# One-hot rows of the first batch turned as words of two tokens, and another order of the queues up to FFN block 1

## The chip, the cores and the metric

The kernel runs on 1 core of one Trainium2 chip. The metric is the time of one execution on the device in microseconds; lower is better. The engines are named as in the profile: PE (TensorE, with its weight loads as PEld), DVE (VectorE), ACT (ScalarE), POOL (GpSimd) and SP (SyncE, which here issues nearly all DMAs).

## The reference

Routed attention in which a query sees only the keys of its own cluster, followed by a feed-forward block (FFN) with a SoLU and a layer norm. There are 4 batches, 8 heads, 768 tokens, head size 64, 16 clusters; the FFN goes from 512 to 1024 and back over 3072 tokens.

```python
q_assign = argmax(einsum('bhsd,hcd->bhsc', q_n, c_n), axis=-1)   # k_assign alike, rows normalised
mask = q_assign[:, :, :, None] == k_assign[:, :, None, :]
scores = np.where(mask, scale * q @ k.T, -1e9)
attn = softmax(scores, axis=-1)
x = (attn @ v) with heads side by side           # 3072 x 512
h = x @ w_in
solu = h * softmax(h, axis=-1)
ln = (solu - mean) / sqrt(var + 1e-6) * g_ln
out = ln @ w_out
```

## The kernel before, in words

**Masking by product.** The mask is not applied afterwards. For each token a one-hot row of its cluster (16 rows, and 32 partitions are kept) is placed under the 64 rows of q and of k in the tiles `qbig` and `kbig`. A score product over 80 partitions then gives q.k/256 plus 1 where the clusters agree, and the exponential (`expo`, line 643, ACT, `scale` 256/8 and `bias` minus that) brings everything else to about zero. So before any score of a pair of heads can be formed, its q and k have to be loaded, turned, cast, assigned to clusters, and their one-hot rows placed.

**Names.** The work is a list of named operations, each with an engine. For batch b and pair p of heads (i is 0 for q, 1 for k):
- `ld b.p.i` loads tokens (SP), `tp` turns them on PE (batch 0 only, two halves of 384 columns into PSUM banks), `xa`/`xt` copies the two halves from PSUM to the tile `xt` (in later batches `xt` is one DVE transpose).
- `ca b.p.i.hh` casts `xt` to bf16 into `qbig`/`kbig` (lines 436 to 440; hh is the head of the pair; pair 0 of batch 0 in halves).
- `cl` multiplies by the centroids on PE (line 469), `tb` turns the result on DVE into `cst` (line 478), `mx` takes the maximum over 16 clusters (line 488), `oh` compares with it and gives the one-hot tile `oh` (line 492), `ot` turns that back into `oht` (lines 499 and 504), `pl` places its rows under q and k (lines 528 and 530, four per item). Pair 0 of batch 0 goes in two items, `0.0` and `0.0.1`, of 192 columns; pairs 1 to 3 of batch 0 are one item of 384 columns each.
- `S r.x` are score products into the PSUM tiles `sb` (line 633), four products a region r; `E r` is the exponential of region r; `V n.j` are the products with the values into the bank `ob` (line 655); `N g` normalises (lines 667 and 678, DVE). In batch 0 the regions S0 to S8 belong to pair 0, and S9, S12 and S15 are the first ones of pairs 1, 2 and 3.
- `lv`/`cv` load and cast v; `lo`/`me`/`mk`/`mf`/`km`/`ce` centre the second weight matrix once (`gt`, `gk`, `gw` prepare g_ln for it); `li` loads the first one. `h`, `hm`, `ex`, `u`, `tu`, `bn`, `y`, `sc`, `ou` are the FFN of one block of 128 tokens, spread between the scores of later batches; `tx` turns its input.

**What sets the order.** One list, `ORDER`, names every operation once; operations are recorded in that order, so each engine's queue is the list with the other engines' names left out. An engine takes its queue strictly in order and stands still when the next operation's inputs are missing. A table, `AWAY`, moves single operations to another engine than their usual one. PE and ACT are tied by a ring: two `sb` tiles of 1024 columns hold scores, so S of region r waits for E of region r-2, and E waits for its S.

**Token order of batch 0.** A partition of the loaded tile holds six neighbouring tokens (6c to 6c+5). Turned by PE, tokens come in groups of 128 with step six. In the `qbig`/`kbig` of batch 0 column j*256 + q*128 + c holds token 6c + 2j + q. A score product takes 128 neighbouring columns as keys; in later batches keys are every sixth column.

Of the kernel before, what the change touches and what calls it, by code (L numbers as in the profile page):

```python
# [38 lines left out]
lc ld0.0.0.0 ld0.0.1.0 ld0.0.0 ld0.0.1 wu ld0.1.0 ld0.1.1 ld0.2.0 cx cy lv0.0 ld0.2.1 tp0.0.0.0 cz  # L39
ld0.3.0 tp0.0.0.1 xa0.0.0 lg tp0.0.1.0 xt0.0.0 ca0.0.0.0.0 lv0.1 cp lo1 ca0.0.0.0.1 cb tp0.0.1.1  # L40
xa0.0.1 ld0.3.1 ca0.0.0.1.0 ca0.0.1.0.0 cl0.0 cc lo2 xt0.0.1 ca0.0.0.1.1 tp0.1.0.0 tb0.0
ca0.0.1.1.0 tp0.1.0.1 mx0.0 xa0.1.0 cl0.0.1 ca0.0.1.0.1 oh0.0 xt0.1.0 tp0.1.1.0 ca0.0.1.1.1 tb0.0.1
ld1.0.0.0 tp0.1.1.1 xa0.1.1 ca0.1.0.0 mx0.0.1 ot0.0 ld1.0.0.1 xt0.1.1 tp0.2.0.0 oh0.0.1 pl0.0.1.1
# [129 lines left out]
def kernel(  # L173
# [15 lines left out]
    P = 128  # L189
# [293 lines left out]
    def each(x, t):  # L483
        return x[:, :wide(t)].rearrange("p (a c) -> p a c", c=NC_)
# [863 lines left out]
```

## Time and profile before

| | |
|---|---|
| Time, median of 3 runs | 221.01 us (220.79 to 221.11) |
| Profiled execution, its own time | 221.75 us |
| Span of that execution in the trace | 219.9 us |
| ACT busy | 191.6 us, 87% of the span |
| DVE busy | 185.4 us, 84% |
| POOL busy | 159.7 us, 73% |
| Granted clock of PE | 1.0 in all stretches |

The time of an execution is a little longer than its span, since the span counts from the first to the last instruction. In rows of the timeline the columns are: start, length in us, engine, line of the kernel, operation, output and input tile with partitions x elements and type, and the number of instructions merged into the row; in brackets the idle time of the engine ahead of the row and who ended it. In rows of groups the number behind the comma is the mean of one instruction in ns. An engine's row can be longer than the time until the next one begins, as neighbouring instructions overlap.

### The profile page before, as it was taken

To read this page: it belongs to the slowest core of one execution; us is meant where nothing else is said; L and a number is where in the kernel's file an instruction comes from. 1 tells how busy PE (TensorE), PEld (TensorE's weight loads), DVE (VectorE), ACT (ScalarE), POOL (GpSimd) and SP (SyncE) were. 2 spreads that over 40 slices of the span, in tenths; PEclk is the share of its full clock that TensorE was granted. 3 is DMA by queue.
4 is the path that set the end of the run, shared out by engine and by line. 5 is a ranking of instruction groups with operands and counts; after the bars stand their busy time and mean duration, and the time that the engine had idled before them with its cause. 6 is when DMAs were issued, how large, how long until landed. Compare 5 with 4: busy or idle time off the path is not lost.

```text
span 219.9 us, 6271 instructions
## 1 busy us (share of the span) xinstructions
PE 210.8 (96%) x2400; PEld 148.0 (67%) x2431; DVE 185.4 (84%) x431; ACT 191.6 (87%) x242; POOL 159.7 (73%) x199
## 2 busy tenths in 40 slices
PE   7799989999999999999999999999999999999993
PEld 4467657777768777877677677666777766655552
DVE  3799989879799999996899999994888756889892
ACT  3599989999999999999999989999999888785471
POOL 3699688859898999649939987979989054456530
PEclk9999999999999999999999999999999999999999
DMA  6995999998199999999989991919474329686613
GB/s 190 381 368 137 281 183 182 169 162 190 23 194 174 208 167 150 217 249 210 185 198 168 190 171 23 221 48 214 140 167 97 84 48 187 137 135 145 190 51 145
DMA packets 120879, 37.28 MB, mean 170 GB/s; under 512 B 109961, under 2 KB 116369, under 8 KB 120849
## 3 DMA queue, kind: packets, MB, share of 16 engines
q1 hardware_dynamic: 119872, 35.31, 77.7%
q0 software_dynamic: 544, 1.05, 2.9%
q10 hardware_dynamic: 432, 0.52, 0.7%
q8 instruction: 19, 0.31, 0.6%
q14 instruction: 12, 0.09, 0.1%
HBM read 23.11 MB, written 6.29 MB: 134 GB/s over the span
## 4 chain that ended last, share of the span: by engine, by line
PE 87%; DVE 6%; DMA 3%; issue 2%; SPq 1%; POOL 0%; ACT 0%; DVEq 0%
PE sb L633 27%; PE hb L766 18%; PE mb L838 16%; PE ob L655 15%; PE hb L469 4%; DMA raw<-in_q_dram 3%; PE hb L395 2%; PE hb L838 2%; DVE oht L504 1%; PE mb L469 1%; DVE mx L488 1%; DVE cst L478 1%; DVE qbig L530 1%; DVE xt L408 1%; PE sb L838 0%
## 5 line engine op out<-in xcount | busy, mean ns | idle before, releaser
L643 ACT ACTIVATE e<-sb 128x1024 bf16<-128x1024 f32 x144 | 140.3, 1022 | 9.8 <-PE sb L633 8.8
L633 PE MATMUL sb<-qbig,kbig 80*128 80x256 bf16 (+3 forms) x648 | 84.9, 261 | 1.0 <-POOL kbig L530 0.4
L633 PEld LDWEIGHTS <-kbig 80*128 80x128 bf16 (+1 forms) x648 | 62.4, 119 | 24.7 <-issue 6.5
L799 POOL TENSOR_TENSOR u<-e_sb,w_st 128x1024 bf16<-128x1024 bf16 x21 | 45.0, 2143 | 18.6 <-ACT e_sb L792 12.1
L655 PEld LDWEIGHTS <-e 128*128 128x128 bf16 x1152 | 48.6, 97 | 12.7 <-issue 2.3
L655 PE MATMUL ob<-v,e 128*128 128x65 bf16 x1140 | 51.8, 193 | 0.4 <-DVE x L678 0.2
L766 PE MATMUL hb<-w_in_sb,xT 128*128 128x512 bf16 x172 | 50.4, 379 | 0.6
L838 PE MATMUL mb<-w_out_c,uT 128*128 128x512 bf16 x157 | 43.6, 379 | 0.6
L810 DVE BATCH_NORM_STATS2 bs<-u 128x6 f32<-128x512 bf16 x48 | 31.8, 681 | 1.1 <-POOL u L799 1.0
L792 ACT ACTIVATE e_sb<-w_st,nmax 128x1024 bf16<-128x1024 f32 (+1 forms) x25 | 27.8, 1113 | 5.5 <-DVE w_st L776 4.1
L438 POOL CAST qbig<-xt 64x768 bf16<-64x768 f32 (+1 forms) x31 | 25.8, 834 | 6.4 <-ACT xt L406 2.2
L440 POOL TENSOR_SCALAR kbig<-xt 64x768 bf16<-64x768 f32 (+1 forms) x30 | 26.7, 894 | 2.2 <-DVE xt L420 0.7
L834 POOL TENSOR_TENSOR alpha<-var,halves 128x1 f32<-128x1 f32 x24 | 15.7, 655 | 11.8 <-DVE var L817 11.2
L420 DVE STREAM_TRANSPOSE xt<-raw 128x768 f32<-128x768 f32 x24 | 22.6, 960 | 0.0
L838 PEld LDWEIGHTS <-uT 128*128 128x128 bf16 x176 | 15.2, 97 | 9.6
L766 PEld LDWEIGHTS <-xT 128*128 128x128 bf16 x192 | 16.1, 98 | 7.9
L776 DVE TENSOR_SCALAR_CACHE_REDUCE w_st<-hb,nmax 128x512 f32<-128x512 f32 x24 | 17.9, 744 | 2.9 <-PE hb L766 2.3
L678 DVE TENSOR_TENSOR x<-ob,den 128x256 bf16<-128x256 f32 (+2 forms) x40 | 19.0, 474 | 1.4
L776 DVE TENSOR_SCALAR_CACHE_REDUCE w_st<-hb 128x512 f32<-128x512 f32 x24 | 16.3, 680 | 3.9 <-PE hb L766 3.8
L667 DVE RECIPROCAL den<-ob 128x4 f32<-128x4 f32 (+2 forms) x40 | 7.2, 180 | 9.7 <-PE ob L655 9.2
L530 POOL COPY qbig<-oht 32x768 f32<-32x768 f32 (+2 forms) x11 | 9.2, 837 | 8.4 <-DVE oht L499 7.3
L530 POOL COPY kbig<-oht 32x768 f32<-32x768 f32 (+2 forms) x17 | 11.1, 654 | 3.2 <-DVE oht L504 2.0
(114 smaller groups left out, 203.0 us busy)
## 6 DMA issues: line engine op xcount, KB each, us to landing
vf<-in_v_dram SPq DMA_DIRECT2D x16, 384.0 KB, 4.9
out_dram<-y SPq DMA_DIRECT2D x20, 256.0 KB, 3.6
raw<-in_k_dram SPq DMA_DIRECT2D x26, 192.0 KB, 3.8
raw<-in_q_dram SPq DMA_DIRECT2D x24, 192.0 KB, 5.1
w_g<-in_moe_w_out_dram SPq DMA_DIRECT2D x4, 512.0 KB, 7.3
raw<-in_q_dram SPq DMA_DIRECT2D x3, 384.0 KB, 7.0
raw<-in_k_dram SPq DMA_DIRECT2D x3, 384.0 KB, 7.4
w_in_sb<-in_moe_w_in_dram POOLq DMA_DIRECT2D x2, 512.0 KB, 7.4
```

Source lines behind the costliest of these rows:

```text
L420: nc.vector.transpose(xts[b, p, i][:], raw_of(b, p, i))
L438: (nc.vector if e == "DVE" else nc.gpsimd).tensor_copy(dst, src)
L440: (nc.vector if e == "DVE" else nc.gpsimd).tensor_scalar(dst, src, scalar1=inv_C, scalar2=1.0, op0=Alu.mult, op1=Alu.mult)
L633: nc.tensor.matmul(reg[:, c:c + wd], kb[u, pp, side_of(h), keys], qb[u, pp, side_of(h), su * P:su * P + wd])
L643: nc.scalar.activation(es[r][:, :w], src, Act.Exp, scale=exp_scale, bias=-exp_scale)
L655: nc.tensor.matmul(ops_of(group_of[n])[:, s, :VW], es[r][:, c0:c0 + P], v1[index[b, pair_of(h)] % R][:, side_of(h), kt, :VW], start=(kt == ...
L766: nc.tensor.matmul(hb[f2][:], xTs[f][:, dc, :], w_in_sb[:, dc, f2 * BANK:(f2 + 1) * BANK], start=(dc == 0), stop=(dc == n_dc - 1))
L776: nc.vector.tensor_scalar(ff[f, "h"][:, f2 * BANK:(f2 + 1) * BANK], hb[f2][:], scalar1=-1.0, scalar2=nmax[:, f2 - 1:f2] if f2 else 3.0e38, ...
L792: nc.scalar.activation(ff[f, "e"][:, cols(f, f2)], ff[f, "h"][:, cols(f, f2)], Act.Exp, bias=ff[f, "nmax"][:, n_ff2 - 1:], scale=-1.0, acc ...
L799: (nc.vector if e == "DVE" else nc.gpsimd).tensor_tensor(ff[f, "u"][:, cols(f, f2)], ff[f, "e"][:, cols(f, f2)], ff[f, "h"][:, cols(f, f2) ...
L810: nc.vector.bn_stats(ff[f, "bs"][:, f2, :], ff[f, "u"][:, f2 * BANK:(f2 + 1) * BANK])
L838: nc.tensor.matmul(y_of(f, x), ff[f, "uT"][:, fc, :], w_out_c[:, fc, parts_of(f, x)], start=(fc == 0), stop=(fc == n_fc - 1))
```

## The change

It has two parts.

**Words of two tokens.** In batch 0 the two tokens 6c + 2j and 6c + 2j + 1 now lie side by side: column j*256 + 2c + q. `oh` writes its one-hot values with the two tokens' bits of a cluster next to each other, so that two bf16 values form one 4-byte word, and `ot` turns words: one transpose of half as many elements in place of two transposes of 2-byte elements. The casts of batch 0 write every second column; score products of batch 0 load every second column as keys; a block of 128 outputs of batch 0 holds 64 pairs of neighbouring tokens, so the store goes by pairs of rows.

```diff
-            dst = (big_[:D, pp, x].rearrange("p (j q a c) -> p a j q c", q=2, a=2, c=D)
+            dst = (big_[:D, pp, x].rearrange("p (j a c q) -> p a j q c", q=2, a=2, c=D)
...
-            dst = big_[:D, pp].rearrange("p h (j q c) -> p h j q c", q=2, c=P)[:, :, :, hh]
+            dst = big_[:D, pp].rearrange("p h (j c q) -> p h j q c", q=2, c=P)[:, :, :, hh]
...
     def assign_hot(t):
         asg[t, "oh"] = pr.tile([P, 2 * HALF], BF16, name="oh")
+        if early(pairs[ITEMS[t][0][0]][0]):
+
+            w = wide(t)
+            nc.vector.tensor_tensor(
+                asg[t, "oh"][:, :w].rearrange("p (k c q) -> p k q c", q=2, c=NC_),
+                asg[t, "cst"][:, :w].rearrange("p (k q c) -> p k q c", q=2, c=NC_),
+                asg[t, "mx"][:, :w // NC_].rearrange("p (k q) -> p k q", q=2).unsqueeze(3)
+                .to_broadcast([P, w // NB, 2, NC_]), op=Alu.is_ge)
+            return
...
-        for x in range(2):
-            nc.vector.transpose(
-                asg[t, "oht"][:, :2 * w].rearrange("p (j q c) -> p j q c", j=n_t // 2, q=2)[:, :, x],
-                asg[t, "oh"][:, :w].rearrange("p (k q c) -> p k q c", q=2, c=NC_)[:, :, x]
-                .unsqueeze(2).to_broadcast([P, w // NB, 2, NC_]))
+        nc.vector.transpose(
+            asg[t, "oht"][:, :2 * w].bitcast(F32),
+            asg[t, "oh"][:, :w].bitcast(F32).rearrange("p (k c) -> p k c", c=NC_)
+            .unsqueeze(2).to_broadcast([P, w // NB, 2, NC_]))
...
-            src = asg[t, "oht"][r, :2 * L].bitcast(F32).rearrange("p (t c) -> p t c", c=NB)
+            src = asg[t, "oht"][r, :2 * L].bitcast(F32).rearrange("p (j c) -> p j c", c=D)
             dst = (big_[D:HOT, pp, c0 // HALF].bitcast(F32)
-                   .rearrange("p (t a c) -> p t a c", a=2, c=NB)[:, :, x])
+                   .rearrange("p (j a c) -> p j a c", a=2, c=D)[:, :, x])
...
-            keys = bass.ts(kt, P) if early(b) else slice(kt, S, n_t)
+            keys = (slice(kt // 2 * 2 * P + kt % 2, (kt // 2 + 1) * 2 * P, 2) if early(b)
+                    else slice(kt, S, n_t))
...
-            dst = out[b * S:(b + 1) * S].rearrange("(p t) m -> t p m", t=n_t)[su]
+
+            dst = (out[b * S:(b + 1) * S].rearrange("(g p j q) m -> j g p q m", g=2, j=n_t // 2, q=2)
+                   [su // 2, su % 2])
+            o = ff[f, "o"][:]
+            eng.dma_start(out=dst.rearrange("p q m -> p (q m)"), in_=o)
+            return
```

**Order and engines.** `ORDER` changes from the first loads up to the scores of batch 1 that run beside FFN block 1 (about S60); behind that every engine's queue is as before. 35 operations change engine, 30 of them in batch 0's preparation:

```diff
-    ca0.0.1.0.0 ca0.3.0.1 ca3.1.1.0 ca3.2.0.1 cv0.0.0 cv0.0.1 cv0.1.1 cv1.1.0 cv1.1.1 cv1.2.0
+    ca0.0.1.0.1 ca0.1.1.0 ca3.1.1.0 ca3.2.0.1 cv0.1.0 cv1.1.0 cv1.2.0 cv1.3.1 cv2.0.1 cv2.1.0
```

To DVE go ca0.0.0.0.0, ca0.0.0.1.0, ca0.0.0.1.1, ca0.1.0.1, ca0.2.0.0, xa0.1.1, xa0.2.0, pl0.0.1.1.1, pl0.1.1.0, pl0.2.0.0, cv0.3.1, ce1 and ce6. To ACT go xt0.0.0, xt0.0.1, xt0.2.1, ca0.0.1.0.1, ca0.1.1.0, cv0.1.0, pl0.0.1.1, pl0.0.0.0, pl0.0.1.1.0 and pl0.2.1.1. To POOL go ca0.0.1.0.0, ca0.3.0.1, pl0.0.1.0, pl0.0.1.0.1, pl0.2.0.1, cv0.0.0, cv0.0.1, cv0.1.1, cv0.3.0, cv1.1.1, ce2 and ce4. On SP the load of g_ln goes ahead of the second k load of pair 2, one load of w_out (lo0) and v of pair 2 go ahead of batch 1's first loads, and v of pair 3 goes ahead of four loads of batch 1's k.

The queue of PE, where the first score products (into `sb_90`) stand between turns of tokens (into the banks `hb_92` and `hb_93`) and pair 1's centroid products (into `mb`). Before:

```order
L395 MATMUL hb_92<-ident_f,raw 128x128 x3
L395 MATMUL hb_93<-ident_f,raw 128x128 x3
L469 MATMUL mb<-xt,g_wide 32x384 x4
L633 LDWEIGHTS kbig_99
L633 MATMUL sb_90<-qbig_96,kbig_99 128x256
```

After, at the same place:

```order
L394 MATMUL hb_92<-ident_f,raw 128x128 x3
L641 LDWEIGHTS kbig_99
L641 MATMUL sb_90<-qbig_96,kbig_99 128x256
...
L468 MATMUL mb<-xt,g_wide 32x384 x4
L394 MATMUL hb_93<-ident_f,raw 128x128 x3
```

The first scores moved ahead of pair 1's centroid products and of one turn of tokens.

The queue of DVE while pair 0's two items are assigned (`cst`, `mx`, `oh`, `oht` as above; `kbig_99` and `qbig_96` are the tiles of pairs 0 and 1). Before:

```order
L478 STREAM_TRANSPOSE cst<-mb 128x192
L488 TENSOR_REDUCE mx<-cst 128x12
L440 TENSOR_SCALAR kbig_99<-xt 64x2x3x64
L492 TENSOR_TENSOR oh<-cst,mx 128x192
L478 STREAM_TRANSPOSE cst<-mb 128x192
L488 TENSOR_REDUCE mx<-cst 128x12
L504 STREAM_TRANSPOSE oht<-oh 128x3x64 x2
L492 TENSOR_TENSOR oh<-cst,mx 128x192
L504 STREAM_TRANSPOSE oht<-oh 128x3x64 x2
L530 COPY qbig_96<-oht 32x6x32
```

After:

```order
L477 STREAM_TRANSPOSE cst<-mb 128x192
L487 TENSOR_REDUCE mx<-cst 128x12
L494 TENSOR_TENSOR oh<-cst,mx 128x6x2x16
L511 STREAM_TRANSPOSE oht<-oh 128x192
L477 STREAM_TRANSPOSE cst<-mb 128x192
L407 COPY xt<-hb_92 128x384
L487 TENSOR_REDUCE mx<-cst 128x12
L494 TENSOR_TENSOR oh<-cst,mx 128x6x2x16
L511 STREAM_TRANSPOSE oht<-oh 128x192
L537 COPY kbig_99<-oht 32x3x64
```

The first item's turn now follows its comparison at once and is one instruction; the cast between left, and a copy of a turned half came in.

The queue of DVE from pair 3's `cst` on, to the placing of its rows (`kbig_100` and `qbig_97` are the tiles of pairs 2 and 3). Before:

```order
L478 STREAM_TRANSPOSE cst<-mb 128x384
L530 COPY kbig_100<-oht 32x384
L667 RECIPROCAL den<-ob 128x4
L678 TENSOR_TENSOR x<-ob,den 128x2x2x64
L488 TENSOR_REDUCE mx<-cst 128x24
L492 TENSOR_TENSOR oh<-cst,mx 128x384
L440 TENSOR_SCALAR kbig_100<-xt 64x6x128
L504 STREAM_TRANSPOSE oht<-oh 128x3x128 x2
L530 COPY qbig_97<-oht 32x384
```

After:

```order
L477 STREAM_TRANSPOSE cst<-mb 128x384
L537 COPY qbig_97<-oht 32x384
L675 RECIPROCAL den<-ob 128x4
L686 TENSOR_TENSOR x<-ob,den 128x2x2x64
L537 COPY kbig_100<-oht 32x384
L487 TENSOR_REDUCE mx<-cst 128x24
L439 TENSOR_SCALAR kbig_100<-xt 64x768
L494 TENSOR_TENSOR oh<-cst,mx 128x12x2x16
L511 STREAM_TRANSPOSE oht<-oh 128x384
L537 COPY qbig_97<-oht 32x384
```

Both placings of pair 2 that DVE does now stand behind `cst` of pair 3, one of them behind a normalisation; the cast of pair 3's keys moved ahead of the comparison, and the turn is one instruction.

More of the change, by code (lines that the diff above doesn't have):

```diff
@@ L35 @@
+    u19.0 u2.0 u21.0 u22.0 u3.0 u4.0 u5.0 u6.0 u7.0 u8.0 u9.0
 """.split(), "POOL"))
 ORDER = """
[L39 to L43, printed above, removed]
```

113 lines of the change are left out of this document (58 added, 55 removed).

## The prediction

> **What bounds the kernel now.** I read the page first, then the busy time of every engine in stretches, then the waits of PE, and last the timeline of each engine around those waits.
>
> ```profile
> span 219.9 us, 6271 instructions
> PE 210.8 (96%) x2400; PEld 148.0 (67%) x2431; DVE 185.4 (84%) x431; ACT 191.6 (87%) x242; POOL 159.7 (73%) x199
> PE 87%; DVE 6%; DMA 3%; issue 2%; SPq 1%; POOL 0%; ACT 0%; DVEq 0%
> ```
>
> PE is busy 96% of the span and carries 87% of the chain that ended last. The change takes no product away from PE, so the gain can be no more than idle time of PE. The table by stretches (columns: length, then busy time and instructions of PE, weight loads, DVE, ACT, POOL) says where that idle time lies:
>
> ```profile
> 5.00:10.00 5.00, 3.82 (x38) 2.56 (x37) 3.69 (x11) 2.91 (x7) 3.35 (x8) 1.00 1.02 365
> 10.00:12.16 2.16, 1.92 (x17) 0.81 (x15) 2.06 (x8) 1.85 (x5) 1.44 (x5) 1.00 1.06 399
> 20.00:25.00 5.00, 4.85 (x70) 2.95 (x68) 4.81 (x13) 4.64 (x7) 3.97 (x7) 1.00 0.99 302
> 25.00:30.00 5.00, 4.58 (x54) 2.68 (x51) 4.78 (x10) 4.56 (x6) 3.25 (x7) 1.00 1.00 161
> 30.00:35.00 5.00, 4.59 (x71) 3.58 (x70) 3.99 (x8) 4.56 (x5) 4.84 (x8) 1.00 1.16 203
> 40.00:45.00 5.00, 4.82 (x67) 3.38 (x67) 4.01 (x9) 4.83 (x6) 3.09 (x4) 1.00 0.99 160
> 50.00:55.00 5.00, 4.95 (x59) 3.71 (x58) 4.61 (x12) 5.00 (x7) 4.64 (x7) 1.00 0.78 173
> 120.00:160.00 40.00, 39.58 (x440) 28.09 (x447) 35.33 (x80) 38.25 (x49) 35.04 (x39) 1.00 0.78 145
> ```
>
> PE idles 1.18 us in 5 to 10, 0.24 in 10 to 12.16, 0.15 in 20 to 25, 0.42 in 25 to 30, 0.41 in 30 to 35 and 0.18 in 40 to 45. From 45 on it loses about 1% (0.42 of 40 us in 120 to 160), and there every queue but the order of a few entries stays as it was. These are the waits behind the sums:
>
> ```profile
> PE ob L655 <- DVE x L678: 0.2, 1, 0.2
> 8.10 0.87 PE L395 MATMUL hb<-ident_f,raw 128*128 128x128 f32 x6 [0.41 <-DMA raw<-in_q_dram]
> 10.48 0.93 PE L395 MATMUL hb<-ident_f,raw 128*128 128x128 f32 x6 [0.24 <-ACT xt L406]
> 12.16 0.60 PE L633 MATMUL sb<-qbig,kbig 80*128 80x256 bf16 x4
> 29.06 0.61 PE L633 MATMUL sb<-qbig,kbig 80*128 80x256 bf16 x4 [0.42 <-POOL kbig L530]
> 33.07 0.60 PE L633 MATMUL sb<-qbig,kbig 80*128 80x256 bf16 x4 [0.32 <-ACT e L643]
> ```
>
> The first scores (S0) start at 12.16. S15, the first scores of pair 3, wait 0.42 us for the keys' one-hot rows (line 530), and at 33.07 S19 waits 0.32 us for an exponential. The 0.41 at 8.10 and the rest of the 1.18 wait for loads of q and k whose issues keep their places: not recoverable. What the change could at most win is 0.24 + 0.15 + 0.42 + 0.41 + 0.18 = 1.4 us.
>
> **The one-hot turn.** S15 waits because DVE is late with pair 3's one-hot rows:
>
> ```profile
> 10.19 0.63 DVE L504 STREAM_TRANSPOSE oht<-oh 128x192 bf16<-128x192 bf16 x2
> 27.24 1.02 DVE L504 STREAM_TRANSPOSE oht<-oh 128x384 bf16<-128x384 bf16 x2
> 7.76 0.38 DVE L478 STREAM_TRANSPOSE cst<-mb 128x192 f32<-128x192 f32 x1
> 17.17 0.57 DVE L478 STREAM_TRANSPOSE cst<-mb 128x384 f32<-128x384 f32 x1
> 28.32 1.24 POOL L530 COPY kbig<-oht 32x384 f32<-32x384 f32 x2 [1.42 <-DVE oht L504]
> ```
>
> The turn of pair 3 ends at 28.26, POOL's placing starts at 28.32, and PE goes at 29.06. Two 2-byte turns become one turn of 4-byte words with half the elements. The nearest rows of that type and size are the f32 turns of line 478: 0.38 us for 192 elements and 0.57 for 384. I take those: 2 x (0.63 - 0.38) + 3 x (1.02 - 0.57) = 1.9 us less on DVE before 28 us. If a word cost as much as two 2-byte elements, nothing would be won; no row speaks for that.
>
> **DVE's moved work.** Between its first cst and pair 3's turn DVE gives away two xt copies, one cast, two placings and gets two xt copies, two 64x768 casts and three placings. The casts before the first cst fall in its idle time.
>
> ```profile
> 19.50 1.01 DVE L530 COPY qbig<-oht 32x384 f32<-32x384 f32 x1
> 23.17 0.35 DVE L530 COPY qbig<-oht 32x384 f32<-32x384 f32 x1
> 26.13 1.19 DVE L440 TENSOR_SCALAR kbig<-xt 64x768 bf16<-64x768 f32 x1
> 19.48 0.83 POOL L440 TENSOR_SCALAR kbig<-xt 64x768 bf16<-64x768 f32 x1
> 25.82 1.08 POOL L440 TENSOR_SCALAR kbig<-xt 64x768 bf16<-64x768 f32 x1
> 11.76 0.25 DVE L530 COPY qbig<-oht 32x192 f32<-32x192 f32 x1
> 8.45 0.60 DVE L440 TENSOR_SCALAR kbig<-xt 64x384 bf16<-64x384 f32 x1
> ```
>
> A placing on DVE takes 0.35 us alone and 1.01 beside a POOL cast that began 0.02 us earlier: it ends 0.20 after POOL. The 64x768 cast that began at 26.13 ended at 27.32, 0.42 after POOL's at 26.90, so 0.42 is its own time. The xt copies cancel. What leaves is a cast (0.60) and two placings (0.25 and 0.35); what comes is 2 x 0.42 and 0.35 + 0.35 + 0.25. That is 1.2 against 1.8, or 0.6 more, at best; each meeting with POOL adds up to 0.66 for a placing and 0.77 for a cast, at most 3.1 for two large placings, one small one (0.25) and two casts. With the shorter turn DVE ends between 1.3 us earlier and 1.8 later. Following the order given under the change, POOL stands still when DVE's two casts come (it waits for an xt copy that ACT now makes after E2), so I count about one meeting: 0.6 us earlier, pair 3's turn at about 27.6 instead of 28.26, and S15 free at about 28.4.
>
> The Trainium skill ("SBUF — State Buffer", section "Who interferes with whom") says that copies and casts of DVE from SBUF to SBUF and POOL share a port pair, and that whichever begins later waits out the other's whole instruction. The two rows at 19.48 and 19.50 agree. By it every one of the moved casts and placings could meet POOL, which is the upper end above.
>
> **PE up to S15.** S0 no longer stands behind cl0.1: oh0.0 is rid of the 0.60 cast before it, its turn follows at once, and its last two placings stand on ACT behind one xt copy. PE can reach S0 at 10.48 + 0.43 = 10.9 (half of the 0.93 row), 1.2 us earlier; but cl0.1 and a turn of tokens then follow, so this is order and no PE time. The 0.24 at 10.48 stays, since the same xt copy is made at the same time by DVE. PE is at S15 at 28.64, its 29.06 less the wait, and finds it free since 28.4: **-0.4 us**. What would be late next there is PE itself.
>
> **ACT.** Its line of exponentials is the partner: 5.00 of 5 us busy in 50 to 55.
>
> ```profile
> 12.85 1.02 ACT L643 ACTIVATE e<-sb 128x1024 bf16<-128x1024 f32 x1
> 13.90 0.51 ACT L553 CAST v<-vf 128x384 bf16<-128x384 f32 x1
> 25.60 0.84 ACT L436 ACTIVATE qbig<-xt 64x768 bf16<-64x768 f32 x1
> ```
>
> Between E0 and E16 it loses a v cast and a 0.84 cast (1.35) and gets an xt copy and a placing. ACT's copies there are priced by the v cast (0.51 for 384 elements), so about 1.0 comes back: 0.3 us less, and E0 comes earlier with S0. S19's wait of 0.32 shrinks but PE comes earlier too; I take **-0.2**. The last 0.1 of 30 to 35 is V10, which waited for a late v load:
>
> ```profile
> 32.85 0.86 DVE L555 CAST v<-vf 128x384 bf16<-128x384 f32 x1
> 27.08 1.59 SPq L547 DMA_DIRECT2D vf<-in_v_dram  x1
> ```
>
> That load's issue (27.08) now goes ahead of four loads of batch 1's keys: **-0.1**. The 0.18 and 0.15 I leave as they are.
>
> **The strided columns.** Casts of the first batch now write every second 2-byte column, on three engines, and scores load keys in steps of two. No row shows such a write. POOL's rows give no sign that packing matters: 64x768 to bf16 takes 0.83. I take nothing, with an upper end of doubling (eight large POOL casts before S15, 6.6 us), which is a rival below. For the loads the rows bracket it:
>
> ```profile
> L633 PEld LDWEIGHTS <-kbig 80*128 80x128 bf16 x152 | 13.4, 98 | 8.1 <-issue 3.8 <-POOL qbig L530 0.6 <-POOL v L555 0.6
> L633 PEld LDWEIGHTS <-kbig 80*128 80x128 bf16 x90 | 10.1, 126 | 4.4 <-issue 1.2
> L633 PE MATMUL sb<-qbig,kbig 80*128 80x256 bf16 x152 | 23.0, 272 | 0.7 <-POOL kbig L530 0.4 <-ACT e L643 0.3
> L633 PE MATMUL sb<-qbig,kbig 80*128 80x256 bf16 x90 | 13.8, 274 | 0.0
> ```
>
> The first and third are of batch 0 (12 to 52 us, adjacent keys), the others of later batches (84 to 140, steps of six): 98 against 126 ns a load, but only 272 against 274 a product. Batch 0 has 144 products, so 0 to 144 x 2 ns = 0.3 us. I take a small part, 0.05. The skill's same page ("Door 1: The DMA port swizzle") calls a step of up to 8 bf16 elements free; steps of six cost 28 ns here, so the measurement decides, and by the page the term would be 0.
>
> **At nothing: stores and other loads.** Batch 0's six stores write pairs of rows; they land under the attention of later batches, and the tail's stores are batch 3's, so they would cost something only if SP's queue ran late by the slack of several us that it has there. DVE now meets batch 1's first xt before km and N4, at about 28.9. Its last load was issued at 22.07 and landed 5.7 us later, at 27.8:
>
> ```profile
> 22.07 1.16 SPq L412 DMA_DIRECT2D raw<-in_q_dram  x1
> DMA to landing us min/median/max: 5.7/5.7/5.7
> ```
>
> The same loads stand ahead of it as before, so I cost the wait at nothing. The cover is 1.1 us; a load later than that holds DVE, behind it km and N4, and through N4 the values of pair 3 on PE.
>
> **Sum.** -0.4 - 0.2 - 0.1 + 0.05 = about -0.7 us. The profiled execution took 221.75 us; less 0.7 is 221.05. It lay 0.74 above the median of 221.01, and a difference carries over: **220.3 us**. The tail and everything past FFN block 1 run as before, and PE there is as full as before, so the lead should last.
>
> **The rivals.**
> - *The lead is not kept, or the wait is only replaced* (220.6 to 221.4, take 220.9). PE's S15 goes at 28.64, but then pair 1's or 2's placings, now on DVE behind the normalisations, hold S9 or S12 by 0.3 to 0.4; or ACT, full from 45 on, lets PE catch up with nothing. For it: a placing that meets POOL takes 1.01. Against: ACT gets lighter too.
> - *Slower: DVE meets POOL.* The place is pair 3's turn, the price 0.66 or 0.77 us a meeting. Three more than the one I count (2 x 0.66 + 0.77 = 2.1) free S15 at 28.4 + 2.1 = 30.5, 1.4 later than the 29.06 of before; less the 0.3 of the other terms that is 1.1 us: 222.1. From 1.0 us of extra waits on the gain is gone (S15 at 29.4), from 1.4 on it is measurably slower. For it: all five moved pieces stand where POOL is busy 3.25 to 3.97 us of 5 today. Against: by the new order POOL itself waits (for ACT's xt copy, and for cl0.3 ahead of widening g) where most of these pieces come. Writes of every second column that take POOL 0.2 us longer each (8 x 0.2) would end in the same place.
> - *More is won* (219.4 to 219.8). All 1.4 us of idle go, because DVE meets nobody and S9, S19 and V10 find all done: 221.01 - 1.4 = 219.6.
> - *The turn by words is no faster.* Then the 1.9 us stay, S15 is free at 28.4 + 1.9 = 30.3, and the time is 221.01 + 1.2 - 0.3 = 221.9; this is counted in the slower case.
>
> **How the numbers follow.** A measurement of this kernel tells about 0.2% (0.44 us) from no change, so faster is below 220.57 and slower above 221.45. The forecast (219.9 to 220.57) has 0.50, more won 0.07, not kept 0.28, slower 0.15. Faster: 0.57, same 0.28, slower 0.15. The range is 219.5 to 221.6: it leaves out the far part of the slower case and little below; the likeliest case alone spans 219.9 to 220.57.
>
> **What would show it.** The turn as one instruction of about 0.57 us for 384 elements; S0 near 10.9 and E0 near 12.0; no wait of PE for kbig at S15; DVE placings of 0.35 rather than 1.0; casts on ACT at 0.84 and on POOL at 0.83 though strided; weight loads of batch 0 between 98 and 126 ns; PE idle in 20 to 35 of about 0.3 instead of 0.98. A cast on POOL well above 0.83, or DVE idle before batch 1's first xt because its load comes late, would make it wrong.

## The result, and the profile after

The changed kernel took 222.76 us (median of 6, 222.46 to 223.05) against 221.16 us for the kernel before on the same chip: ratio 1.0071, 95% interval 1.0053 to 1.0089. It is 0.7% slower, by about 1.6 us, where 0.7 us less was forecast, and outside the range of 219.5 to 221.6. Times and ratios are those of fast executions; where a kernel had single ones that were over 1.5% longer, these are left out.

Of the page of the changed kernel, the span, the busy times and the chain's first line:

```profile
span 221.1 us, 6300 instructions
PE 213.1 (96%) x2431; PEld 148.7 (67%) x2431; DVE 186.5 (84%) x430; ACT 191.6 (87%) x241; POOL 159.7 (72%) x196
PE 83%; DVE 6%; POOL 4%; ACT 3%; issue 2%; DVEq 0%; ACTq 0%; POOLq 0%
```

POOL now carries 4% of the chain that ended last, where it carried 0%. The stretches of the changed kernel (columns as in the prediction), and TensorE's longer waits between 9 and 35 us, with the start of each:

```profile
20.00:25.00 5.00, 4.80 (x69) 3.27 (x71) 4.75 (x12) 4.16 (x5) 4.04 (x7) 1.00 0.78 143
25.00:30.00 5.00, 4.33 (x52) 2.10 (x45) 4.73 (x9) 4.35 (x6) 3.16 (x5) 1.00 1.01 185
30.00:35.00 5.00, 4.64 (x63) 3.58 (x64) 4.12 (x10) 4.23 (x6) 4.81 (x8) 1.00 1.04 166
```

```profile
9.91 0.55 PE L394 MATMUL hb<-ident_f,raw 128*128 128x128 f32 x3 [0.39 <-DVE xt L407]
10.77 0.61 PE L641 MATMUL sb<-qbig,kbig 80*128 80x256 bf16 x4 [0.31 <-POOL kbig L537]
19.11 0.55 PE L394 MATMUL hb<-ident_f,raw 128*128 128x128 f32 x3 [0.43 <-DVE xt L407]
21.71 0.61 PE L641 MATMUL sb<-qbig,kbig 80*128 80x256 bf16 x4 [0.20 <-DVE kbig L537]
30.04 0.61 PE L641 MATMUL sb<-qbig,kbig 80*128 80x256 bf16 x4 [0.71 <-POOL kbig L537]
34.05 0.60 PE L641 MATMUL sb<-qbig,kbig 80*128 80x256 bf16 x4 [0.32 <-ACT e L651]
```

S0 is early (10.77), as forecast, but TensorE then waits at a turn of tokens (19.11), at S9 (21.71) and longest at S15: 30.04, almost 1 us later than the 29.06 of before, and 1.4 us later than forecast. From 20 to 35 it idles 0.20 + 0.67 + 0.36 = 1.23 us; 0.98 was there before and 0.3 was forecast. ScalarE got emptier too (4.16 and 4.35 of 5). The wait of 0.32 us at S19 (34.05) is as long as it was before.

VectorE is why. Its rows and POOL's in the changed kernel, at pair 1's and pair 3's turns:

```profile
15.51 2.52 POOL L439 TENSOR_SCALAR kbig<-xt 64x768 bf16<-64x768 f32 x2 [1.81 <-ACT xt L405]
15.75 1.39 DVE L494 TENSOR_TENSOR oh<-cst,mx 128x384 bf16<-128x384 f32 x1
17.58 0.57 DVE L511 STREAM_TRANSPOSE oht<-oh 128x384 f32<-128x384 f32 x1
26.57 1.05 POOL L439 TENSOR_SCALAR kbig<-xt 64x768 bf16<-64x768 f32 x1
26.63 1.45 DVE L439 TENSOR_SCALAR kbig<-xt 64x768 bf16<-64x768 f32 x1
28.66 0.58 DVE L511 STREAM_TRANSPOSE oht<-oh 128x384 f32<-128x384 f32 x1
```

The turns take 0.57 and 0.58 us as one instruction. But the comparison at 15.75 and the cast at 26.63 each began just behind a POOL cast and took 1.39 and 1.45 us; the same comparison takes 0.58 elsewhere. The last turn ends at 29.24 instead of 28.26, although it alone is 0.44 us shorter.

The kernel before was profiled once more (221.29 us, nearer its median than the first profile's 221.75). Its last turn and its S15:

```profile
26.98 1.01 DVE L504 STREAM_TRANSPOSE oht<-oh 128x384 bf16<-128x384 bf16 x2
28.80 0.61 PE L633 MATMUL sb<-qbig,kbig 80*128 80x256 bf16 x4 [0.41 <-POOL kbig L530]
```

Against it the last turn of the changed kernel ends 1.25 us late (29.24 against 27.99), S15 starts 1.24 us late, and the span is 1.6 us longer (221.1 against 219.5). The exponentials behind S15 tell how this goes on: E15 starts 1.24 us late, E102 1.37 and the last one 1.54. So most of the loss is made before S15 and about 0.3 us behind it, which no run takes apart. From here on this second profile is the one compared with.

### The profile page after: what moved, and what is told of

Its sections match the earlier page's. It is cut to its first block, busy times and chain, and to the rows that moved or that the text cites. A ratio compares the mean times of both kernels' runs of the same rounds, so it can differ in the third digit from the quotient of the medians.

```text
span 221.1 us, 6300 instructions
## 1 busy us (share of the span) xinstructions
PE 213.1 (96%) x2431; PEld 148.7 (67%) x2431; DVE 186.5 (84%) x430; ACT 191.6 (87%) x241; POOL 159.7 (72%) x196
## 4 chain that ended last, share of the span: by engine, by line
PE 83%; DVE 6%; POOL 4%; ACT 3%; issue 2%; DVEq 0%; ACTq 0%; POOLq 0%
PE sb L641 25%; PE hb L774 18%; PE mb L846 16%; PE ob L663 13%; PE hb L468 4%; ACT e L651 3%; DVE xt L419 2%; PE hb L846 2%; PE hb L394 1%; PE sb L954 1%; POOL kbig L439 1%; DVE w_st L784 1%; PE mb L468 1%; POOL qbig L437 1%; DVE xt L407 1%
## 5 line engine op out<-in xcount | busy, mean ns | idle before, releaser
L774 PE MATMUL hb<-w_in_sb,xT 128*128 128x512 bf16 x192 | 53.7, 379 | 0.0
L663 PE MATMUL ob<-v,e 128*128 128x65 bf16 x1140 | 52.4, 193 | 0.0
L846 PE MATMUL mb<-w_out_c,uT 128*128 128x512 bf16 x168 | 45.6, 379 | 0.0
L439 POOL TENSOR_SCALAR kbig<-xt 64x768 bf16<-64x768 f32 (+1 forms) x30 | 27.8, 927 | 3.5 <-ACT xt L405 1.8
L437 POOL CAST qbig<-xt 64x768 bf16<-64x768 f32 (+1 forms) x28 | 24.7, 882 | 6.2 <-PE ob L663 2.1
L537 POOL COPY kbig<-oht 32x768 f32<-32x768 f32 (+2 forms) x13 | 9.9, 763 | 6.3 <-DVE oht L507 3.4
```

What stands on the lines that cost most here:

```text
L437: (nc.vector if e == "DVE" else nc.gpsimd).tensor_copy(dst, src)
L439: (nc.vector if e == "DVE" else nc.gpsimd).tensor_scalar(dst, src, scalar1=inv_C, scalar2=1.0, op0=Alu.mult, op1=Alu.mult)
L663: nc.tensor.matmul(ops_of(group_of[n])[:, s, :VW], es[r][:, c0:c0 + P], v1[index[b, pair_of(h)] % R][:, side_of(h), kt, :VW], start=(kt == ...
L774: nc.tensor.matmul(hb[f2][:], xTs[f][:, dc, :], w_in_sb[:, dc, f2 * BANK:(f2 + 1) * BANK], start=(dc == 0), stop=(dc == n_dc - 1))
L846: nc.tensor.matmul(y_of(f, x), ff[f, "uT"][:, fc, :], w_out_c[:, fc, parts_of(f, x)], start=(fc == 0), stop=(fc == n_fc - 1))
```

## The experiments

Two theories to begin with: W, the layout by words makes casts on POOL and ScalarE slower and so loses the time; O, the new order and engines lose it. Each run's time stands as its ratio to the kernel before on the same chip, with the 95% interval; 0.001 is 0.22 us.

### The two parts apart

`e1_words_only` is the layout by words with the order and engines of before. `e2_order_only` is the order and engines of after with the layout and the turns of before.

```diff
 # e1: the changed kernel with the old lists
-ORDER, AWAY of the changed kernel
+ORDER, AWAY of the kernel before
 # e2: the kernel before with the new lists
-ORDER, AWAY of the kernel before
+ORDER, AWAY of the changed kernel
```

> The layout by words and the one-instruction turn, with the order of all queues and the table of engines as before the change. Theory W (the writes of every second column slow the casts of batch 0 on POOL and ScalarE, and this eats what the turns win): POOL's casts of 64x768 at 1.05 instead of 0.83 us, ScalarE's at 1.06 instead of 0.84, the turns at 0.38 and 0.57; scores of pair 3 (S15) at 29.0 to 30.0 us, time between 0 and 1.0 us above the kernel before. Theory O (the new order and the new engines lose the time: VectorE meets POOL and comes late): the turns' 1.9 us stay won, S15 before 29.0, time 0.2 to 1.0 us below the kernel before.

> The order of all queues and the table of engines of the changed kernel, with the layout and the two-instruction turn of before. Theory W: casts back at 0.83 (POOL) and 0.84 us (ScalarE); S15 within 0.4 us of before's 29.06 and the time within 0.4 us of before, although the turns cost VectorE 1.9 us more. Theory O: oh0.1 and the cast ca0.3.1.0 still take about 1.4 us beside POOL, S15 at 30 to 31, time 1.0 to 2.0 us above the kernel before.

Measured: e1 0.9998 (0.9989 to 1.0008), 221.09 us; e2 1.0142 (1.0128 to 1.0155), 224.24 us. With the changed kernel this makes a square: the new order costs 3.1 us on the old layout (1.0142) and 1.6 on the words (1.0071 against 0.9998). The words are worth 1.6 us in the new order and nothing measurable in the old one. So the time is lost by the order and its engines, as theory O says, and the words don't cause it. Theory O's own numbers missed, though: it had e1 at 0.2 to 1.0 us below the kernel before, and e2 only 1.0 to 2.0 us above it.

Why are the words worth nothing alone? In e1, two comparisons and a placing on VectorE, then S12 and S15 on TensorE:

```profile
14.47 1.16 DVE L495 TENSOR_TENSOR oh<-cst,mx 128x384 bf16<-128x384 f32 x1
22.00 1.17 DVE L538 COPY qbig<-oht 32x384 f32<-32x384 f32 x1
25.30 0.95 DVE L495 TENSOR_TENSOR oh<-cst,mx 128x384 bf16<-128x384 f32 x1
25.90 0.60 PE L642 MATMUL sb<-qbig,kbig 80*128 80x256 bf16 x4 [0.26 <-POOL qbig L438]
28.69 0.60 PE L642 MATMUL sb<-qbig,kbig 80*128 80x256 bf16 x4
```

Of the 1.9 us that the turns won, 0.5 reach the last turn, which ends at 27.49 instead of 27.99: VectorE idles 0.93 us near 12 us, and its three comparisons of 384 elements, 0.55 to 0.56 us each in the kernel before, now fall beside POOL's casts and take 1.16, 0.78 and 0.95 us, 1.2 us more. (The placing at 22.00 costs nothing on balance: another, 1.03 us before, now takes 0.35.) S15 waits for nothing any more, but it starts only 0.1 us before the 28.80 of the kernel before, since S12 now waits 0.26 us for a POOL cast.

### The strided casts

`e5_cast_packed` is the changed kernel with casts that write neighbouring columns; q and k of batch 0 then stand in another order than their one-hots.

```diff
-            dst = big_[:D, pp].rearrange("p h (j c q) -> p h j q c", q=2, c=P)[:, :, :, hh]
+            dst = big_[:D, pp].rearrange("p h (j q c) -> p h j q c", q=2, c=P)[:, :, :, hh]
```

> The changed kernel, but the casts of batch 0 write their columns packed, as before the change, so that q and k of batch 0 stand in an order that the one-hots and the key loads don't share: the outputs of batch 0 are of wrongly paired tokens, the work is the same in number and shape. Theory W: POOL's 64x768 casts at 0.83 instead of 1.05 us, ScalarE's at 0.84, oh0.1 and ca0.3.1.0 shorter by 0.2 to 0.4 us, S15 at or before 29.2, time 0.8 us or more below the changed kernel. Theory O: casts shorter too, but VectorE still meets POOL at oh0.1 and at ca0.3.1.0, S15 at 29.7 or later, time within 0.4 us of the changed kernel.

Groups of casts from 7 to 30 us (mean ns behind the comma), first the changed kernel, then e5:

```profile
L437 POOL CAST qbig<-xt 64x768 bf16<-64x768 f32 x4 | 4.3, 1077 | 0.2
L435 ACT ACTIVATE kbig<-xt 64x768 bf16<-64x768 f32 x1 | 1.1, 1065 | 0.0
L437 DVE CAST qbig<-xt 64x768 bf16<-64x768 f32 x2 | 1.2, 601 | 0.1
```

```profile
L437 POOL CAST qbig<-xt 64x768 bf16<-64x768 f32 x4 | 3.4, 858 | 0.2
L435 ACT ACTIVATE kbig<-xt 64x768 bf16<-64x768 f32 x1 | 0.8, 845 | 0.0
L437 DVE CAST qbig<-xt 64x768 bf16<-64x768 f32 x2 | 1.1, 554 | 0.1
```

A strided cast costs POOL and ScalarE 0.22 us more, VectorE 0.05. Over POOL's eight that is 1.8 us of its time. Yet e5 is at 1.0063 (1.0051 to 1.0075): 0.2 us better than the changed kernel, which is inside the intervals. Theory W got the durations right and their price wrong. Theory O's forecast held: VectorE still met POOL at both places (1.22 and 1.18 us instead of 1.39 and 1.45), and S15 came at 29.77. One reason why so little comes of it: POOL had room for the longer casts, as it stood 1.81 us ahead of those at 15.51. What they cost in the old order (e1) was not tried.

### Taking single meetings away

`e4_cast_early` moves VectorE's cast of 1.45 us to a place where POOL waits. `e3_two_memsets` turns POOL's two casts beside which VectorE was slow into fills with zeros. (In batch 0 the last index of a cast is the token of a pair of neighbours, for both heads.)

```diff
 # e4, in ORDER
 N1
+ca0.3.1.0
...
 S12.1
-ca0.3.1.0
 # e3, in cast()
+        if (b, p, i, hh) in ((0, 2, 1, 0), (0, 3, 1, 1)):
+            nc.gpsimd.memset(dst, 0.0)
```

> The changed kernel with one name moved: VectorE casts ca0.3.1.0 right after N1, where POOL waits, and not after mx0.3, where it ran beside POOL's ca0.3.1.1 for 1.45 us. Theory O (meetings on VectorE): the cast takes about 0.6 us, the last turn ot0.3 ends near 28.4 instead of 29.24, S15 near 29.3 instead of 30.04, time 0.5 to 0.8 us below the changed kernel. Theory W alone: POOL's casts of 1.05 us still end S15's keys; POOL's last cast ends near 27.6 as now, so S15 moves by under 0.4 us and the time by under 0.3.

> The changed kernel with two of POOL's casts (ca0.2.1.0 and ca0.3.1.1: keys of pairs 2 and 3, one token of each two) left out; POOL fills their columns with zeros instead, so these keys are zero. It reads nothing there. Theory M (the time is lost where VectorE's comparison and cast wait out a POOL instruction that reads and writes SBUF): oh0.1 back from 1.39 to 0.56 us and ca0.3.1.0 from 1.45 to about 0.6, the turn ot0.3 ends near 27.6 instead of 29.24, S15 near 28.7, time 0.9 to 1.4 us below the changed kernel. Theory N (any POOL instruction there holds VectorE, or VectorE is late for another reason): both stay above 1.1 us, time within 0.3 us.

Measured: e4 1.0079 (1.0067 to 1.0091), e3 1.0081 (1.0066 to 1.0097): no gain. In e4 the cast took 0.59 us, but the comparison that now stood beside POOL took the wait over; in e3 the comparison was short (0.57), but the two casts ahead of it took 2.31 instead of 1.23, and the cast of pair 3 waited for the fill. First e4, then e3:

```profile
22.88 0.59 DVE L439 TENSOR_SCALAR kbig<-xt 64x768 bf16<-64x768 f32 x1
27.07 1.05 POOL L439 TENSOR_SCALAR kbig<-xt 64x768 bf16<-64x768 f32 x1
27.25 1.27 DVE L494 TENSOR_TENSOR oh<-cst,mx 128x384 bf16<-128x384 f32 x1
```

```profile
14.37 2.31 DVE L439 CAST qbig<-xt 64x768 bf16<-64x768 f32 x2
26.59 0.96 POOL L435 MEMSET kbig<- 64x768 bf16 x1
26.67 1.33 DVE L441 TENSOR_SCALAR kbig<-xt 64x768 bf16<-64x768 f32 x1
```

So a POOL instruction that only writes holds VectorE's cast as well, and a meeting that is dodged falls on VectorE's next operation of that kind. The Trainium skill ("SBUF — State Buffer", section "Who interferes with whom") says that VectorE in its two-port mode shares a port pair with POOL, and that whichever of the two began later is blocked for the whole of the other's instruction. The cast of 1.33 us ended 0.45 behind the fill, which agrees. Whether a comparison waits for a fill wasn't tried, since none stood beside one.

### Table against order

`e6_table_back` is the changed kernel with the engines of before, `e7_table_new` is e1 with the engines of after, `e8_two_casts_back` gives two of VectorE's casts back to POOL, into POOL's idle 1.81 us.

```diff
 # e8, in the table for "DVE"
-    ca0.0.0.1.1 ca0.1.0.1 ca0.2.0.0 ca0.3.1.0 ce6 cv0.3.1 km mk pl0.1.0.0 pl0.1.1.0 pl0.2.0.0
+    ca0.0.0.1.1 ca0.3.1.0 ce6 cv0.3.1 km mk pl0.1.0.0 pl0.1.1.0 pl0.2.0.0
```

> The changed kernel (layout by words, new order) with the table of engines of before. Theory T (the table costs the time: it gives VectorE casts and placings of batch 0 that POOL did, and in the new order VectorE has no time for them): at least 0.8 us below the changed kernel's 222.8, with tp0.3.1.0's wait for VectorE gone. Theory Q (the order of the queues costs it, whoever does the operations): 222.3 us or more.

> The layout by words with the order of before (e1_words_only) and the table of engines of the changed kernel. Theory T: at least 0.8 us above e1_words_only's 221.1, VectorE without its idle 0.93 us near 12 us and late at the last turn. Theory Q: within 0.4 us of 221.1.

> The changed kernel with two casts, ca0.1.0.1 and ca0.2.0.0, back from VectorE to POOL, which stands idle for 1.81 us at that place (13.7 to 15.5 us). Theory T: VectorE is 0.8 to 1.2 us earlier at the turn ot0.1 (17.58 in the changed kernel), PE's wait of 0.43 us at tp0.3.1.0 goes, S15 at 29.0 to 29.6 instead of 30.04, time 0.5 to 1.0 us below the changed kernel. Theory Q: POOL's two casts of 1.05 us push its queue back in the place of VectorE's, time within 0.3 us of the changed kernel.

Measured: e6 1.0103 (1.0089 to 1.0117), e7 1.0307 (1.0285 to 1.0329), e8 1.0072 (1.0060 to 1.0085). e6 and e7 contradict each other as tests of the theories (e6 came out as Q said, e7 as T said): either new part with the other's old one is worse than both together. In e7 the longest wait of TensorE is for a cast of v, far behind S15. Below it is a row of the stretches:

```profile
36.87 1.22 PE L663 MATMUL ob<-v,e 128*128 128x65 bf16 x24 [1.97 <-POOL v L562]
```

```profile
38.00:39.00 1.00, 1.00 (x8) 0.69 (x6) 0.84 (x3) 0.00 (x0) 0.00 (x0) 0.50 1.34 211
```

Right behind that wait the clock granted to TensorE fell: it was 0.61 from 37 to 38 us, 0.50 from 38 to 40 and 0.68 from 40 to 41, then 1.00 again. All five executions of e7 show a mean clock of 0.985 to 0.992, so part of its 3% is this lower clock and not the order of the work.

e8 is clean, and theory T missed: VectorE gave 1.2 us of casts away ahead of pair 1's turn, but its last turn ended only 0.2 us earlier (29.00). Its rows show where the rest went. VectorE reached pair 1's turn 1.3 us earlier (16.27 instead of 17.58) and pair 2's cst 1.1 us earlier. Then pair 1's placing on VectorE, 0.35 us in the changed kernel, met a POOL cast, and the comparison behind it took 0.75 instead of 0.58:

```profile
19.94 1.05 POOL L439 TENSOR_SCALAR kbig<-xt 64x768 bf16<-64x768 f32 x1
20.24 1.08 DVE L537 COPY kbig<-oht 32x384 f32<-32x384 f32 x1
```

### The early start of S0

`b0_before_again` is the kernel before. `e11_products_first` is the changed kernel with cl0.1 and tp0.2.0.1 ahead of S0 on TensorE again; no other queue changes.

```diff
+cl0.1
+tp0.2.0.1
 S0.0
...
-cl0.1
...
-tp0.2.0.1
```

> The kernel before once more, for a second profile of it: whether its waits of PE for the loads of q and k (0.8 and 0.4 us at 6 to 8 us in the first) come again. If the loads land at a time of their own in each execution, these waits differ by some tenths of a us from run to run and the time with them, 220.8 to 221.8 us; if the order of the loads sets them, they are the same to 0.1 us.

> The changed kernel with pair 1's centroid products (cl0.1) and one turn of tokens (tp0.2.0.1) ahead of S0 on TensorE again, as before the change; nothing else moves. If the lead of S0 is mere order and VectorE pays for it (it waited 0.35 us for cl0.1): S0 and E0 about 1.1 us later, VectorE's wait of 0.35 gone, the turn ot0.3 0.2 to 0.4 us earlier and the time 0.2 to 0.4 us below the changed kernel. If the early exponentials are worth something, ScalarE is late instead: 0.3 us or more above it.

Measured: the second profile of before has waits for loads of 0.3 us only, where the first had 0.77 and 0.41; so these land at a time of their own in each execution, and the first profile was probably late by about 0.3 us for that reason. e11: 1.0043 (1.0029 to 1.0057), 222.12 us, 0.6 us better than the changed kernel (0.2 to 0.4 were expected; the interval of the difference is about 0.5 to either side). The last turn ends at 28.62 instead of 29.24, S15 starts at 29.42 instead of 30.04. Pair 1's products on TensorE and its cst on VectorE, first the changed kernel, then e11:

```profile
11.31 0.85 PE L468 MATMUL mb<-xt,g_wide 128*32 128x384 f32 x8
12.26 0.58 DVE L477 STREAM_TRANSPOSE cst<-mb 128x384 f32<-128x384 f32 x1 [0.35 <-PE mb L468]
```

```profile
10.56 0.85 PE L468 MATMUL mb<-xt,g_wide 128*32 128x384 f32 x8
12.01 0.57 DVE L477 STREAM_TRANSPOSE cst<-mb 128x384 f32<-128x384 f32 x1
15.43 0.57 DVE L494 TENSOR_TENSOR oh<-cst,mx 128x384 bf16<-128x384 f32 x1
```

VectorE no longer waits 0.35 us, and its comparison of pair 1, now 0.3 us earlier, is in front of POOL's pair of casts: 0.57 instead of 1.39. The lead of S0 was paid for on VectorE. Two operations moved here, pair 1's products and a turn of tokens, and no run separates them.

### The rest of the loss

What is left, 1.0043, was taken apart on top of e11: e12 gives the two casts back to POOL, e13 also the copy xa0.2.0 to ScalarE, e14 (on e13) and e15 (on e11) bring pair 2's products forward, e16 (on e13) moves the copy xa0.3.0 ahead of N0, and e17 also gives the placing pl0.1.1.0 back to POOL.

```diff
 # e12: off the table for "DVE"
-ca0.1.0.1 ca0.2.0.0
 # e13: and in the table for "ACT"
+xa0.2.0
 # e14, e15: xt0.2.1 back to DVE behind tp0.2.1.1, N0 behind tb0.2, and
 tp0.3.0.0
+cl0.2
 # e16
 oh0.1
+xa0.3.0
 ot0.1
+N0
 # e17: off the table for "DVE", behind pl0.1.0.1 on POOL
-pl0.1.1.0
```

> e11_products_first with the two casts ca0.1.0.1 and ca0.2.0.0 back on POOL as well. If the rest of the loss is work moved to VectorE: the turn ot0.3 0.5 to 1.0 us earlier than e11's 28.62 and the time 0.3 to 0.8 us below e11's 222.12. If POOL is the late one by then, or meetings eat it: within 0.2 us of 222.12.

> e12_both_back with one copy of a turned half (xa0.2.0, 0.56 us) back from VectorE to ScalarE, where it falls between ScalarE's last placing and E0. If VectorE's work is the rest of the loss: another 0.2 to 0.5 us below e12, and near the 221.1 of the kernel with the words alone. If not: within 0.2 us of e12.

> e13_copy_back with the copy xt0.2.1 on VectorE as before the change, pair 2's centroid products cl0.2 ahead of V0 and S3, and the normalisation N0 behind the turn ot0.1 and tb0.2. If the late products are the rest of the loss: cl0.2 at about 14.5 instead of 16.2, tb0.2 at 15.5 to 16.5 instead of 17.2, the turn ot0.3 at least 0.6 us before e13's 28.87, the time 0.5 to 0.9 us below e13's 222.09. If VectorE's and POOL's meetings hold pair 3 whatever the order: within 0.2 us of 222.09.

> The same three moves on top of e11_products_first, where VectorE keeps the two casts and the copy xa0.2.0 and so has some 2.3 us of work more than in e14 ahead of pair 2's turn. If late products alone are the rest: 0.5 us or more below e11's 222.12. If they matter only with VectorE free to use them: within 0.3 us of 222.12, since cl0.2's result waits in its bank.

> e13_copy_back with the copy xa0.3.0 moved ahead on VectorE into its idle 0.55 us before N0, and the turn ot0.1 ahead of N0. If the gapless stretch of VectorE behind tb0.2 sets S15: that stretch is 0.5 us shorter (11.2 instead of 11.7), S15 and E15 0.3 to 0.5 us earlier (E15 near 30.0 instead of 30.38), the time 0.3 to 0.5 us below e13's 222.09. If something else sets it: within 0.2 us.

> e16_copy_early with the placing pl0.1.1.0 (1.09 us on VectorE beside a POOL cast in e13) back on POOL, behind pl0.1.0.1. If the stretch behind tb0.2 sets S15: another 0.4 to 0.9 us shorter, S9 no later, the time 0.3 to 0.8 us below e16 and near the 221.1 of the words alone. If a meeting only moves on to VectorE's next operation, or pair 3's products on TensorE hold it: within 0.2 us of e16.

Measured: e12 1.0064 (1.0048 to 1.0079), e13 1.0045 (1.0033 to 1.0058), e14 1.0081 (1.0069 to 1.0093), e15 1.0169 (1.0136 to 1.0202), e16 1.0046 (1.0032 to 1.0059), e17 1.0039 (1.0025 to 1.0053). None is better than e11 by more than its interval. e14 and e15 were misses: bringing pair 2's products forward made it worse. In e14 VectorE twice waits 0.68 us for turns of tokens (at 13.25 and 14.48); in e15 its two casts take 2.32 us instead of 1.23, and TensorE waits 1.49 us for a normalisation.

The others show where the time goes instead. Pair 2's cst on VectorE, in the second profile of before and in the changed kernel:

```profile
16.89 0.57 DVE L478 STREAM_TRANSPOSE cst<-mb 128x384 f32<-128x384 f32 x1
```

```profile
18.07 0.54 DVE L477 STREAM_TRANSPOSE cst<-mb 128x384 f32<-128x384 f32 x1
```

From there to the end of the last turn VectorE takes 11.10 us before and 11.17 after. So of the 1.25 us by which the last turn is late, 1.18 are lost ahead of pair 2's cst; and behind it nothing is won, although two turns there are 0.9 us shorter in sum, since VectorE also has four copies there instead of two and four placings instead of three (and two normalisations instead of three). In e11, e12 and e13 this cst starts at 17.17 to 17.19, whatever was taken off VectorE ahead of it. In e11 the last turn is still 0.63 us late: 0.29 of it ahead of this cst and 0.34 behind. VectorE and TensorE in e13, then TensorE in e17:

```profile
13.16 0.56 DVE L407 COPY xt<-hb 128x384 f32<-128x384 f32 x1 [0.65 <-PE hb L394]
15.89 0.18 DVE L675 RECIPROCAL den<-ob 128x4 f32<-128x4 f32 x1 [0.55 <-PE ob L663]
20.11 1.09 DVE L537 COPY kbig<-oht 32x384 f32<-32x384 f32 x1
29.68 0.61 PE L641 MATMUL sb<-qbig,kbig 80*128 80x256 bf16 x4 [0.72 <-POOL kbig L537]
```

```profile
28.81 0.60 PE L641 MATMUL sb<-qbig,kbig 80*128 80x256 bf16 x4
```

Ahead of pair 2's cst, work taken off VectorE in e13 became waits for TensorE (0.65 and 0.55 us). Behind it VectorE has little gap up to the last turn (0.52 of 11.71 us in e13), so what leaves that stretch should count; e16 and e17 try it. e16 took a copy out of it, but a placing that had cost 0.35 us met POOL and took 0.77. e17 took the placing of 1.09 us out: in its trace S15 starts at 28.81 without a wait (28.80 in the kernel before). But this was e17's fastest execution (221.44 us; its median is 221.98), so what its other executions lose is not seen and stays open.

### A version faster than both

e1 pointed to idle time on VectorE and late work on POOL. `e9_words_dve_cast` is e1 with one cast moved from POOL into VectorE's idle time and a zeroing of v on POOL behind the first placings; `e10_words_both` also moves one v cast from ScalarE to POOL.

```diff
 # e9 and e10: table "DVE"
+ca0.1.0.1
 # e9 and e10: ORDER
 tb0.1
+ca0.1.0.1
...
 pl0.0.1.0.0
+z1
 # e10 alone: off the table for "ACT", on POOL where ca0.1.0.1 stood
-cv0.0.1
```

> The layout by words with the order and engines of before (e1_words_only), but the cast ca0.1.0.1 goes from POOL to VectorE, right behind tb0.1 where VectorE stood idle 0.93 us, and POOL's zeroing of a piece of v (z1) goes behind the placings of pair 0. If what the turns won lies idle on VectorE at 12 to 13 us while POOL is the late one (S0 waits 0.5 and S12 0.3 us for it), POOL is 1.0 us earlier from 14 us on, both waits shrink, and the time is 0.3 to 0.5 us below e1_words_only's 221.09. If ScalarE's row of exponentials, which had no gap of its own from 14 to 20 us, is the bound, it stays within 0.2 us of 221.09.

> As e9_words_dve_cast, and the cast of v cv0.0.1 (0.51 us between E0 and E1) goes from ScalarE to POOL. If ScalarE is the bound between E0 and E8: E1 at 13.5 instead of 14.0, and 0.3 to 0.5 us below e9. If TensorE is (5.00 of 5 us busy from 15 to 20), no more than 0.2 us below e9.

Measured: e9 0.9987 (0.9969 to 1.0005), 220.84 us; e10 0.9978 (0.9966 to 0.9990), 220.61 us against 221.14. e10 is faster than both kernels, by about 0.5 us against before. Its profile is of an execution of 220.16 us, better than its median. From 15 to 30 us in it TensorE is busy throughout (a row of the stretches, then S15 from the timeline):

```profile
15.00:30.00 15.00, 15.00 (x200) 10.30 (x197) 13.56 (x30) 14.44 (x17) 13.99 (x22) 1.00 0.89 203
```

```profile
27.90 0.61 PE L642 MATMUL sb<-qbig,kbig 80*128 80x256 bf16 x4
```

This is the effect that the change was forecast to have: S15 starts at 27.90 without a wait, 0.9 us earlier than in the kernel before. S19 still waits 0.32 us here too.

## Why the prediction was wrong

- **The turns** were right: one instruction of 0.57 us for 384 elements and 0.38 for 192.
- **VectorE's moved work** is the step that failed first: "0.6 more, at best", "about one meeting", the last turn at 27.6. It ended at 29.24. The stretch from pair 0's cst to the end of the last turn, and the copies of turned halves in it (VectorE is the third engine of each row of a stretch; the other rows are groups), in the second profile of before and in the changed kernel:

```profile
7.50:27.99 20.49, 19.80 (x235) 13.17 (x236) 19.75 (x45) 18.74 (x26) 16.39 (x30) 1.00 1.05 289
```

```profile
L408 DVE COPY xt<-hb 128x384 f32<-128x384 f32 x7 | 3.8, 557 | 0.3
```

```profile
7.50:29.24 21.74, 20.41 (x241) 13.51 (x241) 20.36 (x43) 18.75 (x25) 15.94 (x29) 1.00 1.02 283
```

```profile
L407 DVE COPY xt<-hb 128x384 f32<-128x384 f32 x8 | 4.4, 548 | 0.2
```

  The stretch grew by 1.25 us: 0.61 of it busy, and 0.64 of it gaps (0.74 before, 1.38 after). Three things were mis-sized. "The xt copies cancel" was a miscount: two of the three copies that left VectorE lie before this stretch, so it has 8 instead of 7, 0.55 us more. A 64x768 cast of its own takes 0.60 us and not 0.42, twice. And the meetings: the prediction priced them for the casts and placings that moved and left the comparisons out; one took 1.39. (The second profile of before has one too: 0.64 us at 8.67 for 192 elements instead of 0.34.)

  Against the sum, 0.6 us less forecast and 1.25 more measured, this is about 1.85 us to account for: some 0.5 for the copies, 0.4 for the two casts, 0.7 for comparisons, 0.3 for the old cast that now met POOL for longer (1.45 instead of 1.19) and 0.64 for gaps, less the some 0.7 that the prediction had allowed for one meeting. The new placings came out as priced.
- **"This is order and no PE time"** is the second step that failed. Putting cl0.1 and a turn of tokens behind S0 costs TensorE nothing but starves VectorE by 0.35 us and moves its comparison beside a POOL cast: 0.6 us by e11, the one change of the new order that paid.
- **The strided columns at nothing** was wrong as a duration (0.22 us a cast on POOL and ScalarE, where "POOL's rows give no sign" was read as no cost), but worth only about 0.2 us in time, inside the intervals (e5). The key loads were right: 98 ns a load in batch 0 as before.
- **ACT, -0.2, and S19**: S15's delay emptied ScalarE, so this term never came up. S19 waits 0.32 us in every profile looked at, e10's too, where S15 is on time: that wait doesn't shrink with what this change does, and the term had no row that showed it would. The other term of this kind, 0.1 for V10, rested on a short wait of the first profile that the second doesn't show.
- **The baseline**: of the 1.18 us that TensorE idles from 5 to 10 us in the first profile, the second shows 0.68. What was called not recoverable varies by some tenths from one execution to the next.
- **The rival** "DVE meets POOL" named the mechanism and the place, and gave 222.1 us for three more meetings. It had 0.15. Its argument against, that POOL itself waits where the pieces come, held for the two casts (1.23 us for two) and failed for the comparison behind them. The rival also put S15 at 30.5, later than it came (30.04); still the time was 0.7 us longer than its 222.1, since the terms that it took off for the rest did not come and some 0.3 us is lost behind S15. But its price per meeting is no price in time: e1 has a meeting of 1.17 us and is not slower, and e3 and e4 show that a meeting taken away comes back on the next operation.

What is shown: the order and engines lose the time, the words don't (e1, e2); 0.6 us of it is the place of pair 1's products and one turn of tokens, moved together (e11). What is not settled: the other 1.0 us. The strided casts explain little of it at most (e5); taking a single meeting away gave nothing (e3, e4), nor did the two casts and the copy (e8, e12, e13). By e11's trace some of it lies ahead of pair 2's cst, some in the copies and placings that VectorE has behind it, and the rest behind S15. Of the placings e17's trace points to pair 1's, but its median does not confirm it.

## What to carry to other kernels

As far as these traces tell, time freed on an engine is worth something only in the stretch in which that engine has no gap up to the wait that ends last: count a moved operation there, and ask of each operation ahead of it what fills the hole. When VectorE and POOL work side by side, price not one meeting but the list of VectorE's operations from SBUF to SBUF that can be hit, since the hit moves along it. And here few moves on top of the change that freed time did better than an order made anew: the words with three small moves on the old order (e10) beat both kernels.

## What the runs showed of the hardware

- A cast from float32 to bf16 that writes every second 2-byte column takes POOL 1.08 instead of 0.86 us and ScalarE 1.07 instead of 0.85 for 64x768, but VectorE only 0.60 instead of 0.55.
- A POOL fill, which reads nothing, holds VectorE's cast like a POOL cast does (1.33 us instead of 0.6).
- Comparisons of 128x384 on VectorE were held too: 1.16 and 1.27 us (e1, e4) and 1.39 (changed kernel) beside POOL casts, 0.57 ahead of them (e11).
- Turns on VectorE were never held by POOL: 0.55 to 0.58 us for 384 words in the runs looked at, POOL busy or not.
- Weight loads in steps of two bf16 elements take 98 ns, as neighbouring ones do; steps of six take 126 ns.
- After TensorE had waited 1.97 us in e7, the clock granted to it was 0.50 to 0.68 for about 4 us; elsewhere in that profile's 25 to 36 us it was 1.00.
